# First expert's weights used whole in float32, and squares and casts issued a step or two later, in an attention, expert and gated-network kernel

## The chip, the cores and the metric

The kernel runs on one NeuronCore of a Trainium2 chip. The metric is the device time of one execution in microseconds (us). The engines are TensorE (PE; its weight loads are the row PEld), VectorE (DVE), ScalarE (ACT), GpSimd (POOL) and SyncE (SP, which here issues most of the DMAs).

## The reference: what is computed

Three stages in a row, float32 in and out.

```python
# 1. attention, B=2, H=8, S=576, D=64, causal, with a decay bias from s
scores = q @ k.T / sqrt(D) + min(-(cum[i] - cum[j]), 0)     # cum = cumsum(max(s, 0))
x = softmax(scores) @ v                                      # then 1152 tokens of 512
# 2. eight experts, top 1, capacity 288
expert = argmax(x @ w_gate); gate = softmax(x @ w_gate)[expert]
y = gate * (relu(x @ w1[expert]) @ w2[expert])               # w1 512x1024, w2 1024x512
# 3. gated network
h = y @ w_in                                                 # 512x2048
out = (h * sigmoid(h)) @ w_out                               # 2048x512
```

## The kernel before, in words

**Precision.** PE multiplies float16 here, and accuracy is kept by splitting: each float32 matrix is scaled by a power of two and split into a float16 part (hi, a cast) and the float16 rest (lo, one DVE instruction that scales and subtracts). A product is three float16 products: hi x hi, hi x lo, lo x hi. The scale comes from the sum of squares: ScalarE squares the matrix with a row sum (`w_norm`, line 132, and `w_norm2`, line 139), PE sums over partitions with a matrix of ones (`ones_sum`, L144), DVE reduces and makes the scale from the exponent bits (L146, L100 to L102).

**Attention and routing.** 56 items (a block of queries, a head, one or both batches) pass through a pipeline of steps: scores on PE in float32 (L346, L354), row minimum on DVE (L369), exponent on ScalarE (L387), split (L406 to L411), a transposing DMA (L419), the product with v (L438 to L454). Nine tiles of 128 tokens are then split (`r_split`), transposed on PE (`r_tr`, L530, copied by ScalarE at L531), multiplied with the gate weights (`r_logits`, L539 to L541), reduced to a one-hot of the best expert (`r_top`, L547 to L550), ranked (`r_pos`, L574; `r_rank`) and scattered by an indirect DMA into a table in DRAM that has a region for every expert (`r_scat`, L639). `tail` lists by hand what each engine does in the last part, tiles 6 to 8, in the order in which it is queued. Expert 0's window (its first W = 192 tokens, transposed) is not read back after the last scatter: it is read before, and the tokens of the last three tiles are added by one-hot matmuls (`win_start`, `win_mm`, `win_oh`, `win_add`, L628) and copied to `xw0` (L634, L636). `tail` also splits the first weight (`w_split0`, four parts, L202 on ScalarE and L203 on DVE) and the second (`w_split`, L165, L169, L171), and `warm` gives PE work without a result.

**Experts.** Sixteen weights are used in the order w1 of 0, w1 of 1, w2 of 0, w1 of 2, w2 of 1, ... (`WSEQ`), each 2 MB; a weight's place in it is j. Unit u is PE's work with weight u: four steps q = 0 to 3. In a w1 unit every step makes two blocks of 128 rows of the hidden layer (24 matmuls of 192 columns, `mm_h`, L749); in a w2 unit steps 0 and 2 make two blocks of the output each (48 matmuls, `mm_y`, L779). Results leave PSUM a step later: `post_h` (relu on ScalarE L755, lo part on DVE L756) and `post_y` (DVE scales by the gates into `ys`, L788, and ScalarE squares that with a sum, L791). `flush` issues them. Beside these steps unit u prepares weight j = u + 2 and n = u + 3, and loads weight u + 4:

```python
if q == 0: w_scale(j); flush(); hi(j) on ACT, DVE, POOL    # L185, L187
if q == 1: flush(); w_norm2(n, first half);  w_lo(j, first half)
if q == 2: flush(); w_norm2(n, second half); w_lo(j, second half)   # L139, L192
```

`hi(j)` is half on ScalarE (L185), a quarter on DVE and a quarter on POOL (L187). `unit0` is written out by itself and squares, casts and splits weight 2 (expert 0's w2). Staging buffers hold three weights (`wst` two, `wst2` one, by j mod 3), and the split ones three (`wsp` one, `wsp2` two). All engines' orders are by hand here (`manual_schedule`), and each engine works its queue in order.

**Gates.** Outputs are scaled by the gate of every token slot. `slots0` (DVE, L677 to L682) makes table rows from the totals, nine indirect DMAs on POOL gather the slots' data (`slots_g`, L685), `slots1` (DVE, at the start of unit 2, L692 to L700) makes the gates, SP writes them to DRAM (`gl`, L701) and reads them back to all partitions (`load_gates`, L890). From unit 3, step 2, on `post_y` is issued.

**Second network.** Its weights come as float64 words, which DVE converts in integer arithmetic (`c_conv`, L841 to L843); ScalarE squares them (`c_sq`, L849), `c_scale` makes the scale, POOL and DVE split (`c_split`, L872, L873). `c_tasks` makes a list of these; from unit 6 on two entries a unit are issued (`task`, in steps 0 and 3), the others between the matmuls of the second network (L1111, L1130), whose order a planner sets from modelled times.

Of the kernel before, what the change touches and what calls it, by code (L numbers as in the profile page):

```python
# [23 lines left out]
P = 128  # L24
# [3 lines left out]
W = 192  # L28
# [8 lines left out]
def moe_kernel(tc, qL, qtL, kL, vL, sL, wgL, w1L, w2L, capL, winL, woutL, out):  # L37
# [73 lines left out]
    NW = len(WSEQ)  # L111
    wd = [dict() for _ in range(NW)]
    pools = {}

    def w_load(j, part=None, q=SP):
# [3 lines left out]
        if part in (None, 0):  # L119
            pool = pools["wst2"] if j % 3 == 2 else wst_p  # L120
            wd[j]["st"] = pool.tile([P, 4096], F32, tag="wst", name="wst")
# [72 lines left out]

    def w_split0(f):

        d = wd[0]
        if f == 0:
            d["sp"] = wsp_p.tile([P, 2, 4096], F16, tag="wsp", name="wsp")
        v = d["st"].rearrange("p (k f) -> p k f", k=4)[:, :, f * 256:(f + 1) * 256]  # L200
        o = d["sp"].rearrange("p c (k f) -> p c k f", k=4)[:, :, :, f * 256:(f + 1) * 256]
        A.activation(out=o[:, 0], in_=v, func=AF.Copy, scale=d["s"])  # L202
        V.scalar_tensor_tensor(out=o[:, 1], in0=v, scalar=d["s"], in1=o[:, 0], op0=ALU.mult, op1=ALU.subtract)  # L203
# [401 lines left out]
    xw0 = cst.tile([P, 8, W], F16, name="xw0")  # L605
# [9 lines left out]
    def win_mm():  # L615
        a = win["a"]
        for k in range(4):
            pw.append(psS.tile([P, 512], F32, tag="s", name="pw"))
            PE.matmul(out=pw[k][:, 0:2 * W].rearrange("p (a w) -> p a w", w=W), lhsT=ident16,
                      rhs=a[:, 2 * k:2 * k + 2, :], start=True, stop=False)  # L620
# [4 lines left out]
    def win_add(t):  # L625
        o = oh0[:, t - T0, :]
        for k in range(8):
            PE.matmul(out=pw[k // 2][:, k % 2 * W:(k % 2 + 1) * W], lhsT=rt[t]["xh"][:, k * P:(k + 1) * P], rhs=o,  # L628
                      start=False, stop=(t == NT - 1 and k % 2 == 1))
            if t == NT - 1 and k % 2:  # L630
                j = k // 2
                src, dst = pw[j][:, 0:2 * W], xw0[:, k - 1:k + 1, :].rearrange("p a w -> p (a w)")
                if j % 2:
                    A.copy(dst, src)  # L634
                else:
                    V.tensor_copy(dst, src)  # L636
# [84 lines left out]
    def moe_phases():  # L721
# [15 lines left out]
        hh, posts, yposts = {}, [], []  # L737

        def mm_h(e, fp):
            if fp == 0:  # L740
                hh[e] = hp.tile([P, 2, 8, W], F16, tag="h", name="h")
            sp = wd[wi(("w1", e))]["sp"].rearrange("p c (k f) -> p c k f", k=4)
# [295 lines left out]
        for u in range(1, 4):  # L1038
            unit(u)
            if u == 1:  # L1040
                w_load(5)
# [391 lines left out]
```

## Time and profile before

| | us |
|---|---|
| median of 3 runs | 551.32 (548.91 to 554.57) |
| the profiled execution | 548.38 |
| its span, first to last instruction | 546.7 |
| mean granted clock of PE over the span | 0.93 |

The span is what all times of the trace are counted in; 1.7 us of the profiled execution lie around it. In the trace expert 0's first matmul starts at 156.9 us, unit 1 at 166.25, unit 2 at 179.9, the gates arrive at 204.6, the last expert matmul ends at 332.4, and the second network takes the rest. The rows further down give start and length in us; a wait is told with what released it.

### The profile page before, as it was taken

How to read it: one execution, taken by the hardware profiler on the slowest of the kernel's cores; microseconds unless marked ns; L12 is line 12 of the kernel's file. 1: busy time of each engine (PE TensorE's matmuls, PEld its weight loads, DVE VectorE, ACT ScalarE, POOL GpSimd, SP SyncE). 2: the span in 40 equal slices, each digit the busy share in tenths (PEclk: the TensorE clock that was granted, in tenths of full speed). 3: DMA queues.
4: the chain of work that ended last, by engine and by line, in shares of the span. 5: the costliest groups of instructions: out<-in, count | busy, mean ns of one | idle time of the engine just before them, and what ended most of it. 6: DMA issues, size and time to landing. Idle time of an engine off the chain costs nothing.

```text
span 546.7 us, 10734 instructions
## 1 busy us (share of the span) xinstructions
PE 450.2 (82%) x4094; PEld 364.7 (67%) x4095; DVE 391.6 (72%) x920; ACT 279.0 (51%) x500; POOL 223.2 (41%) x251
## 2 busy tenths in 40 slices
PE   0948678997686967986769897598999989999995
PEld 0735435675586966976669795264588866668885
DVE  8889579985778757879887889998567874452111
ACT  1665466974387557856845723555533245551000
POOL 9787485655127311100121105564542224562121
PEclk9979789998798997989697898899999999999999
DMA  9899999999359639896549601304032430000101
GB/s 160 225 178 215 219 215 249 244 235 232 114 195 340 239 91 313 255 381 190 186 155 233 259 1 42 114 2 155 0 118 66 161 122 1 0 1 20 59 40 58
DMA packets 97126, 83.10 MB, mean 152 GB/s; under 512 B 70112, under 2 KB 74400, under 8 KB 96816
## 3 DMA queue, kind: packets, MB, share of 16 engines
q1 hardware_dynamic: 93840, 75.50, 53.2%
q0 software_dynamic: 1728, 4.76, 2.4%
q10 hardware_dynamic: 1504, 2.13, 1.4%
q8 instruction: 33, 0.54, 0.4%
q14 instruction: 21, 0.17, 0.1%
HBM read 58.07 MB, written 7.91 MB: 121 GB/s over the span
## 4 chain that ended last, share of the span: by engine, by line
PE 38%; DVE 26%; DMA 15%; ACT 7%; issue 7%; POOL 4%; DVEq 0%; POOLq 0%; SPq 0%; ACTq 0%
PE psh L1111 13%; PE psy L1130 9%; DMA eT<-hl 7%; PE psh L749 4%; PE psy L779 4%; DVE wsp L192 4%; DMA gl<-gk 2%; ACT junk L139 2%; DVE cx L842 2%; DVE wsp L309 2%; PE pss L346 2%; DVE stg L843 2%; DVE et L369 2%; DMA stg<-in_moe_w_out_dram 2%; DVE hl L411 2%
## 5 line engine op out<-in xcount | busy, mean ns | idle before, releaser
L1111 PE MATMUL psh<-yh,win 128*128 128x384 f16 x576 | 98.3, 332 | 10.1 <-DVE r L1118 8.5
L1130 PE MATMUL psy<-wout,g 128*128 128x256 f16 x864 | 95.4, 273 | 3.7 <-ACT ot L1138 2.5
L1130 PEld LDWEIGHTS <-g 128*128 128x128 f16 x864 | 84.5, 98 | 14.0 <-issue 4.1
L1111 PEld LDWEIGHTS <-win 128*128 128x128 f16 x576 | 57.3, 100 | 49.9 <-issue 8.4
L749 PE MATMUL psh<-xw,wsp 128*128 128x192 f16 x768 | 75.5, 265 | 1.1 <-DVE h L756 1.1
L749 PEld LDWEIGHTS <-wsp 128*128 128x128 f16 x768 | 72.4, 108 | 2.4 <-DMA xw<-table 1.3
L192 DVE SCALAR_TENSOR_TENSOR wsp<-wst,sci,wsp 128x2048 f16<-128x2048 f32 x28 | 65.5, 2344 | 4.5 <-POOL wsp L187 2.8
L779 PE MATMUL psy<-h,wsp 128*128 128x192 f16 x768 | 68.3, 251 | 0.4 <-DVE wsp L192 0.4
L779 PEld LDWEIGHTS <-wsp 128*128 128x128 f16 x768 | 66.0, 101 | 0.9 <-DVE wsp L192 0.7
L346 PE MATMUL pss<-kt,qa 65*128 65x128 f32 (+3 forms) x128 | 51.2, 549 | 18.5 <-DMA kt<-wsp 12.4
L1120 POOL TENSOR_TENSOR g<-r,g 128x384 f16<-128x384 f32 x48 | 46.8, 978 | 43.7 <-ACT g L1119 42.2
L187 POOL TENSOR_SCALAR wsp<-wst,sci 128x1024 f16<-128x1024 f32 x13 | 15.5, 1196 | 109.7 <-DVE sci L102 60.5
L1118 DVE SCALAR_TENSOR_TENSOR r<-psh,sg 128x384 f32<-128x384 f32 x48 | 26.4, 553 | 32.4 <-ACT sg L1116 31.1
L139 ACT ACTIVATE junk<-wst 128x2048 f16<-128x2048 f32 x26 | 49.4, 1898 | 0.1
L411 POOL TENSOR_TENSOR hl<-et,hl 128x512 f16<-128x512 f32 (+3 forms) x34 | 37.7, 1116 | 18.0 <-ACT hl L406 15.3
L346 PEld LDWEIGHTS pss<-kt,qa 128*128 128x128 f32 (+1 forms) x128 | 26.3, 251 | 28.0 <-POOL qa L261 12.0
L387 ACT ACTIVATE et<-et,nm 128x128 f32<-128x128 f32 (+3 forms) x64 | 32.8, 554 | 21.4 <-DVE nm L369 21.4
L1119 ACT CAST g<-r 128x384 f16<-128x384 f32 x48 | 24.4, 510 | 33.0 <-DVE r L1118 33.0
L185 ACT ACTIVATE wsp<-wst,sci 128x2048 f16<-128x2048 f32 x14 | 27.9, 1996 | 23.2 <-DVE sci L102 17.7
L1140 DVE SCALAR_TENSOR_TENSOR ot<-psy,inv,ot 128x256 f32<-128x256 f32 x18 | 8.7, 484 | 37.4 <-PE psy L1130 37.4
L872 POOL TENSOR_SCALAR win<-stg,sci 128x512 f16<-128x512 f32 x16 | 15.7, 998 | 48.1 <-DVE sci L102 48.1
L369 DVE CUSTOM_DVE_ANT_0 et<-pss,mk 128x128 f32<-128x128 f32 (+3 forms) x64 | 28.9, 480 | 3.7 <-POOL hl L411 3.2
(247 smaller groups left out, 839.2 us busy)
## 6 DMA issues: line engine op xcount, KB each, us to landing
wst<-in_moe_w_dram SPq DMA_DIRECT2D x61, 512.0 KB, 5.9
stg<-in_moe_w_in_dram SPq DMA_DIRECT2D x16, 512.0 KB, 5.8
stg<-in_moe_w_out_dram SPq DMA_DIRECT2D x16, 512.0 KB, 4.9
table<-xh SPq DMA_DIRECT2D x4, 774.0 KB, 6.1
wst<-in_v_dram SPq DMA_DIRECT2D x2, 1024.0 KB
kt<-in_k_dram SPq DMA_DIRECT2D x3, 512.0 KB, 8.4
qa<-in_q_dram SPq DMA_DIRECT2D x3, 512.0 KB, 7.2
wst<-in_moe_w_dram ACTq DMA_DIRECT2D x3, 512.0 KB, 3.2
```

The lines of the kernel that those rows point to most:

```text
L139: A.activation(out=pools["junk2"], in_=d["st"][:, h * 2048:(h + 1) * 2048], func=AF.Square, accum_out=d["ss"][:, h:h + 1])
L185: A.activation(out=o, in_=src, func=AF.Copy, scale=d["s"])
L192: V.scalar_tensor_tensor(out=d["sp"][:, 1, lo:hi], in0=d["st"][:, lo:hi], scalar=d["s"], in1=d["sp"][:, 0, lo:hi], op0=ALU.mult, op1=ALU.s ...
L346: PE.matmul(out=pv[:, j, :], lhsT=qa[c % 2][r, h, b, :], rhs=kt[r, h, b, 0:n], start=True, stop=True)
L369: maxi[i] = V.tensor_tensor_reduce(out=ev[:, j, :], in0=st[i]["s"][:, j, :], in1=mk[:, 512 - n:512], scale=-0.125, scalar=3.0e38, op0=ALU. ...
L387: A.activation(out=e[:, j, :], in_=e[:, j, :], func=AF.Exp, scale=-1.0, bias=st[i]["m"][j])
L411: spl[i] = (V if LO[i] == "V" else G).tensor_tensor(out=hl[:, w:w + n], in0=e, in1=hl[:, 0:n], op=ALU.subtract)
L749: PE.matmul(out=pv[:, j, :], lhsT=sp[:, cw, k, a], rhs=xw[e][:, 4 * cx + k, :], start=(n == 0 and k == 0), stop=(n == 2 and k == 3))
L779: PE.matmul(out=pv[:, j - js[0], :], lhsT=sp[:, cw, k, a], rhs=hh[e][:, ch, k, :], start=(n == 0 and k == 0), stop=(n == 2 and k == 7))
L1111: PE.matmul(out=ps[:, 0:CH], lhsT=wv[:, cw, k, fo * P:(fo + 1) * P], rhs=yh[:, cy, k, a], start=(i == 0 and k == 0), stop=(i == 2 and k == 3))
L1120: G.tensor_tensor(out=gt[n][:, 1, f, :], in0=r, in1=gt[n][:, 0, f, :], op=ALU.subtract)
L1130: PE.matmul(out=o, lhsT=gt[n][:, cg, k, a], rhs=woutt[h][:, cw, k, d], start=(m == 0 and k == 0), stop=(m == 2 and k == 7))
```

## The change

The first expert's two weights (places 0 and 2, `WHOLE`) are no longer squared, scaled, cast and split. They are loaded into buffers of the split weights' pools and multiplied as they are, in float32: 4 matmuls for a block of the hidden layer instead of 12, and 8 for a block of the output instead of 24. `xw0` and the hidden layer of expert 0 are float32, `win_mm` and `win_add` sum hi and lo of the window into one PSUM region, and the copies out of it are two instead of four. Since weight 2 no longer takes a staging buffer, weight 3 is loaded where weight 2 was, weight 2 later, and weight 5 in unit 0 instead of after unit 1.

In all units the cast `hi(j)` is issued in step 1 instead of 0, the halves of `w_lo(j)` in steps 2 and 3 instead of 1 and 2, and the first half of `w_norm2(n)` in step 0 instead of 1. The square of an output is issued by a list of its own, `late`, at least one step after its scaling, and the square of a conversion one task later than its conversion.

```diff
+    WHOLE = (0, 2)
...
+            if j in WHOLE:
+                t = (wsp_p if j == 0 else pools["wsp2"]).tile([P, 2, 4096], F16, tag="wsp", name="wsp")
+                wd[j]["st"] = t.rearrange("p c f -> p (c f)").bitcast(F32)
...
-    def w_split0(f):
...
-    xw0 = cst.tile([P, 8, W], F16, name="xw0")
+    xw0 = cst.tile([P, 4, W], F32, name="xw0")
...
         def mm_h(e, fp):
...
+                if e == 0:
+                    for k in range(4):
+                        PE.matmul(out=pv[:, j, :], lhsT=sp[:, k, a], rhs=xw0[:, k, :], start=(k == 0), stop=(k == 3))
+                    continue
...
         def post_h(e, fp, pv):
+            if e == 0:
+                A.activation(out=whole_h()[:, 2 * fp:2 * fp + 2, :], in_=pv, func=AF.Relu)
+                return
...
         def mm_y(e, dp):
...
+                    if e == 0:
+                        for k in range(8):
+                            PE.matmul(out=pv[:, j - js[0], :], lhsT=sp[:, k, a], rhs=whole_h()[:, k, :],
+                                      start=(k == 0), stop=(k == 7))
+                        continue
...
             V.scalar_tensor_tensor(out=o, in0=pv, scalar=KY[:, e:e + 1], in1=g, op0=ALU.mult, op1=ALU.mult)
+            late.append((now[0], lambda: post_y2(e, d, n)))
+
+        def post_y2(e, d, n):
+            o = ys[:, d:d + n, ds(offv[e], W)]
...
         def c_tasks(m, j):
-            t = []
+            t = [[] for _ in range(5)]
             for q in range(4):
-                t.append([lambda q=q: c_conv(m, j, q), lambda q=q: c_sq(m, j, q)])
-            t.append([])
+                t[q].append(lambda q=q: c_conv(m, j, q))
+                t[q + 1].append(lambda q=q: c_sq(m, j, q))
...
-            for p in posts, yposts:
-                while p and (p is posts or gates) and (not keep or p[0][0] < now[0]):
+            for p in posts, yposts, late:
+                while p and (p is not yposts or gates) and (not keep or p[0][0] < now[0] - (p is late)):
...
             step(0, 0)
-            w_load(3, 1, A)
-            w_load(3, 2)
-            w_load(3, 3)
+            for q in range(1, 4):
+                w_load(2, q)
             for t in range(NT):
                 slots_g(t)
-            w_norm(2, 2)
-            w_norm(2, 3)
             w_load(4)
             step(0, 1)
             flush()
+            w_norm2(3, 0)
+            w_load(5)
             step(0, 2)
-            w_scale(2)
             flush()
-            w_hi(2, 0, 2048, A)
-            w_hi(2, 2048, 4096, V)
+            w_norm2(3, 1)
             step(0, 3)
             flush()
-            w_lo(2, 0, 2048)
-            w_norm2(3, 0)
-            w_norm2(3, 1)
-            w_lo(2, 2048, 4096)
...
                 flush()
-                if q == 0 and j < NW:
+                if q == 0 and n < NW:
+                    w_norm2(n, 0)
+                if q == 1 and j < NW:
                     w_hi(j, 0, 2048, A)
                     w_hi(j, 2048, 3072, V)
                     w_hi(j, 3072, 4096, G)
-                if q == 1:
-                    if n < NW:
-                        w_norm2(n, 0)
-                    if j < NW:
-                        w_lo(j, 0, 2048)
                 if q == 2:
                     if n < NW:
                         w_norm2(n, 1)
                     if j < NW:
-                        w_lo(j, 2048, 4096)
+                        w_lo(j, 0, 2048)
+                if q == 3 and j < NW:
+                    w_lo(j, 2048, 4096)
...
-        w_split0(0)
...
-        w_split0(1)
...
-        w_split0(2)
...
-        w_split0(3)
-        w_load(2, 2, A)
-        w_norm(2, 0)
+        w_load(3, 2, A)
```

## Rows read from the trace of the kernel before

**Rows 1.** The page, part 1: busy us (share of the span) and instructions.
```profile
PE 450.2 (82%) x4094; PEld 364.7 (67%) x4095; DVE 391.6 (72%) x920; ACT 279.0 (51%) x500; POOL 223.2 (41%) x251
```

**Rows 2.** Windows: start:end, length, busy by engine, PE clock, DMA share, GB/s.
```profile
139.50:145.20 5.70, 5.57 (x48) 4.40 (x47) 3.96 (x19) 2.52 (x4) 0.00 (x0) 0.50 0.24 91
...
217.70:318.70 101.00, 83.05 (x888) 81.04 (x889) 82.64 (x116) 63.78 (x88) 13.81 (x13) 0.88 0.71 225
318.70:332.30 13.60, 13.60 (x168) 13.60 (x166) 11.92 (x25) 5.63 (x17) 0.00 (x0) 1.00 0.01 1
...
351.00:450.00 99.00, 92.20 (x701) 68.78 (x702) 76.17 (x137) 47.34 (x108) 41.82 (x43) 0.98 0.25 86
```

**Rows 3.** Waits of the whole span: us in total, times, longest.
```profile
ACT stg L849 <- DVE stg L843: 35.4, 21, 5.9
...
PE psn L144 <- ACT junk L139: 29.2, 9, 7.2
...
ACT junk L791 <- DVE yg L788: 21.1, 14, 5.1
```

**Rows 4.** Chain that ended last, in the tail: start us, us, what.
```profile
137.37 1.28 DVE wsp L203
...
146.69 1.18 DVE wsp L203
...
150.98 1.16 ACT wsp L202
152.17 1.28 DVE wsp L203
```

**Rows 5.** Timeline of POOL, the first of nine gathers.
```profile
164.93 1.02 POOL L685 DMA_INDIRECT meta<-table,srow  x1 [4.54 <-DVE srow L682]
```

**Rows 6.** Chain that ended last, from the last gather to unit 7.
```profile
180.04 0.95 POOL meta L685
...
186.50 0.24 DVE gk L700
186.76 13.44 DMA gl<-gk
200.25 4.38 DMA yg<-gl
...
208.59 0.60 PE psn L144 x2
...
237.55 7.90 DMA wst<-in_moe_w_dram
```

**Rows 7.** Timeline of PE: start, us, operation, count [idle before].
```profile
12.74 4.26 PE L346 MATMUL pss<-kt,qa 65*128 65x128 f32 x19
...
96.33 2.82 PE L346 MATMUL pss<-kt,qa 128*128 128x512 f32 x6
...
104.17 2.26 PE L354 MATMUL pss<-kt,qa 128*128 128x288 f32 x8
...
139.63 0.17 PE L574 MATMUL psm<-oh,tri 128*128 128x8 f16 x1 [2.36 <-DVE oh L550]
...
156.91 6.10 PE L749 MATMUL psh<-xw,wsp 128*128 128x192 f16 x72
```

**Rows 8.** Groups of DVE from 217.7 to 318.7: busy us, mean ns, idle before.
```profile
L192 DVE SCALAR_TENSOR_TENSOR wsp<-wst,sci,wsp 128x2048 f16<-128x2048 f32 x18 | 42.2, 2344 | 0.4 <-ACT wsp L185 0.4
L187 DVE TENSOR_SCALAR wsp<-wst,sci 128x1024 f16<-128x1024 f32 x9 | 12.3, 1368 | 0.0
L756 DVE SCALAR_TENSOR_TENSOR h<-psh,h 128x384 f16<-128x384 f32 x19 | 10.5, 552 | 6.6 <-ACT h L755 6.6
L788 DVE SCALAR_TENSOR_TENSOR yg<-psy,KY,yg 128x384 f32 x9 | 5.6, 618 | 0.1
```

**Rows 9.** Waits from 217.7 to 318.7 us.
```profile
PE psn L144 <- ACT junk L139: 18.0, 6, 7.2
...
DVE sc L146 <- PE psn L144: 6.9, 6, 2.5
```

More of the change, by code (lines that the diff above doesn't have):

```diff
@@ L119, in w_load @@
         if part in (None, 0):
-            pool = pools["wst2"] if j % 3 == 2 else wst_p
-            wd[j]["st"] = pool.tile([P, 4096], F32, tag="wst", name="wst")
+            if j in WHOLE:
+                t = (wsp_p if j == 0 else pools["wsp2"]).tile([P, 2, 4096], F16, tag="wsp", name="wsp")
+                wd[j]["st"] = t.rearrange("p c f -> p (c f)").bitcast(F32)
+            else:
+                pool = pools["wst2"] if j % 3 == 2 else wst_p
+                wd[j]["st"] = pool.tile([P, 4096], F32, tag="wst", name="wst")
         v = wd[j]["st"].rearrange("p (a f) -> p a f", a=n)
@@ L193, in w_lo @@
                                in1=d["sp"][:, 0, lo:hi], op0=ALU.mult, op1=ALU.subtract)
-    def w_split0(f):
[L197 to L203, printed above, removed]
     actx = ExitStack()
@@ L616, in win_mm @@
         a = win["a"]
-        for k in range(4):
+        for k in range(2):
             pw.append(psS.tile([P, 512], F32, tag="s", name="pw"))
-            PE.matmul(out=pw[k][:, 0:2 * W].rearrange("p (a w) -> p a w", w=W), lhsT=ident16,
-                      rhs=a[:, 2 * k:2 * k + 2, :], start=True, stop=False)
+            for c in range(2):
+                PE.matmul(out=pw[k][:, 0:2 * W].rearrange("p (a w) -> p a w", w=W), lhsT=ident16,
+                          rhs=a[:, 4 * c + 2 * k:4 * c + 2 * k + 2, :], start=(c == 0), stop=False)
     def win_oh(t):
@@ L626, in win_add @@
         o = oh0[:, t - T0, :]
[L627 to L633, printed above, removed]
+        for i, k in enumerate((0, 1, 4, 5, 2, 3, 6, 7)):
+            c = k % 4
+            PE.matmul(out=pw[c // 2][:, c % 2 * W:(c % 2 + 1) * W], lhsT=rt[t]["xh"][:, k * P:(k + 1) * P], rhs=o,
+                      start=False, stop=(t == NT - 1 and i % 4 == 3))
+            if t == NT - 1 and i % 4 == 3:
+                j = i // 4
+                src, dst = pw[j][:, 0:2 * W], xw0[:, 2 * j:2 * j + 2, :].rearrange("p a w -> p (a w)")
+                if j:
+                    V.tensor_copy(dst, src)
+                else:
                     A.copy(dst, src)
-                else:
-                    V.tensor_copy(dst, src)
     def r_scat(t):
@@ L736, in moe_phases @@
         wint = [win_p.tile([P, 2, 2, 2048], F16, name=f"win{i}") for i in range(2)]
-        hh, posts, yposts = {}, [], []
+        hh, posts, yposts, late = {}, [], [], []
         def mm_h(e, fp):
@@ L1005, in unit @@
             e = WSEQ[u][1]
-            if u + 4 < NW:
-                w_load(u + 4) if u > 1 else None
+            if u + 4 < NW and u > 1:
+                w_load(u + 4)
             if WSEQ[u][0] == "w1" and 1 <= e < E - 1:
@@ L1046, in moe_phases @@
         extra += [[lambda: c_load("in", 0)]] + c_tasks("in", 0) + [[]]
-        extra += [[lambda: c_load("in", 1)], [lambda: c_load("out", 0)], []] + c_tasks("in", 1)[0:4]
+        extra += [[lambda: c_load("in", 1)], [lambda: c_load("out", 0)], []] + c_tasks("in", 1)[0:5]
         for u in range(4, NW):
@@ L1269, in early @@
                     w_load(j, s - WL[j])
-            if WL[j] + 5 <= s < WL[j] + 9:
+            if WL[j] + 5 <= s < WL[j] + 9 and j not in WHOLE:
                 w_norm(j, s - WL[j] - 5)
-            if s == WL[j] + 8:
+            if s == WL[j] + 8 and j not in WHOLE:
                 w_scale(j)
@@ L1296, in tail @@
         win_start()
-        w_load(2, 0)
-        w_load(2, 1)
+        w_load(3, 0)
+        w_load(3, 1)
         i_pv(49)
@@ L1346, in tail @@
         r_top(8)
-        w_load(3, 0)
+        w_load(3, 3)
         r_pos(8)
```

20 lines of the change are left out of this document (14 added, 6 removed).

## The prediction

> **What bounds the kernel now.** The page's first part comes first: PE is busy for 82% of the span, VectorE (DVE) for 72%, ScalarE (ACT) for 51% [rows 1]. No engine is full, so the loss is in waits, and the windows tell where. In the body of the expert stage (217.7 to 318.7 us, units 5 to 13) DVE works 82.6 of 101.0 us and PE 83.1, at a granted clock of 0.88; the last 13.6 us are PE alone, full and at 1.00 [rows 2]. Third, the list of waits. PE's largest is its weight-norm matmul (L144) waiting for ScalarE's squares of weights (L139): 29.2 us in 9 waits. ScalarE itself sits 21.1 us in front of the squares of outputs (L791) and 35.4 us in front of the squares of conversions (L849), each time for a DVE result issued in the same step [rows 3]. So a wait of ScalarE for DVE becomes one of PE, since the weight squares are queued behind it. Last, the chain of waits. Ahead of the experts it runs through expert 0's split (L202 on ScalarE, L203 on DVE) [rows 4]; then through nine gathers on POOL, the gate write (13.44 us) and its broadcast (4.38 us), to 204.7, when the first output can be scaled, and through L144 at 208.59 [rows 5, 6].
>
> **The tail before expert 0.** Four ScalarE casts and four DVE splits of expert 0's first weight go. Three places of them are on the path. The split at 137.37 stands in DVE's queue ahead of tile 6's routing: PE waited 2.36 us for its one-hot [rows 4, 7]. Right after that wait the granted clock is 0.50 (1.2 of 2.4 GHz) from 139.5 to 145.2, while PE is full (5.57 us) [rows 2]; without the wait I take these matmuls at 1.00, half of it: 2.7 us. The split at 146.69 costs 1.2 us ahead of tile 8's split. Cast and split from 150.98 to 153.45 stand ahead of tile 8's routing, whose logits are there some 1.5 us before the split ends. The window is copied out of PSUM in two pieces instead of four: 0.4 us. Sum 2.4 + 2.7 + 1.2 + 1.5 + 0.4 = 8.2; I take 8. If the clock falls all the same it is 5.5, and it can hardly be more than 8.5: what comes late next is the transposes of the attention weights, which nothing here touches. Expert 0 then starts at 148.9 instead of 156.9.
>
> **Float32 products.** A float32 matmul leaves two records. Start to start (a row's length less that of its last record, over the rest), records of 288 columns come every (2.26 - 0.41)/7 = 0.265 us and of 512 every (2.82 - 0.59)/5 = 0.446, so 0.81 ns a column; 192 columns make 0.265 - 96 x 0.81 ns = 0.187 us. Records of 128 columns with 65 rows come every (4.26 - 0.42)/18 = 0.213, which would make 0.265 for 192 [rows 7]. A unit of expert 0 is 32 float32 matmuls, 64 records: 12.0 us by the first, 17.0 by the second. The 96 float16 records it replaces take 96 x (6.10 - 0.25)/71 = 7.9. I take 12.0, the price of records that use all 128 rows as these do: 4.1 us more in each of two units, 9.1 as the upper end. Expert 0's units then end at 160.9 and, after unit 1, at 181; unit 3 ends at 189, the first half of unit 4 at 193.
>
> The Trainium skill speaks against this edit: "TensorE: Matmul & The Clock Gate", section "Weight-path perf modes", says that float32 weights get no fast load, and its section on what overlaps says that a load runs beside a matmul only when the row groups differ. By its section "LDWEIGHTS", 128 columns / 1.2, a load is 107 ns (an estimate by that page); with 192 x 0.81 = 156 ns of streaming a record would take 263 ns and a unit 17 us. The 288-column records disagree: of their 265 ns, 233 are streaming at that price, so only 32 are left for a load. The 65-row records agree (213 ns, 104 of them streaming). It is the third rival below.
>
> **The gates.** The nine gathers start once DVE has made the rows from the totals, right behind the tail, and hold POOL from 164.93 to 181.0 [rows 5, 6]; all move with the tail, by 8 us (5.5 to 8.5, as it does). POOL's cast of weight 3 stays behind them, and with it DVE's second half of that split, but this now ends at 176.6 (174.2 when the cast is done, plus 2.34 [rows 8]), ahead of the gathers' landing near 178. So the gates leave at 178.8, not 186.76, and with the same 13.44 + 4.38 us arrive at 196.7. That expert 0's second weight is neither squared, cast nor split is worth nothing by itself: units 1 and 2 gain, but PE waits at 193 for the gates in any case. This wait of some 4 us also swallows most of the float32 price.
>
> **Units 3 to 5.** Output squares a step or two later let the weight squares go ahead of them, so PE does not wait at L144 (208.59 now): its second half of unit 4 starts at 197.4, when the first output is scaled. DVE, which sat idle behind that scaling, has then to do: two scalings (1.1), four half splits (9.2), two output splits (1.0), scale and cast (1.5), offset and scaling (0.9): 13.8 us, so it stands at 210.5 where it stood at 217.7: 7 us ahead.
>
> **Units 5 to 13.** DVE's own work is unchanged: 82.6 us, over half of it the 18 half splits of 2344 ns [rows 2, 8]. Its idle time there is 18.4 us: 6.9 for the norm matmul on PE, which waited 18.0 for ScalarE [rows 9], 6.6 for relus [rows 8], the rest small. With squares later and the first weight square a step earlier PE's wait mostly goes; DVE's cast of the next weight is a step later too and finds its scale ready. What comes next is DVE itself; a full DVE holds ScalarE at the cast (its scale comes from DVE), and the second weight square is behind it. I leave 10 us idle (5 at best, 18.4 if the coupling stays): 210.5 + 82.6 + 10 = 303, against 318.7. PE's 9 units of 8 us fit in that.
>
> **The end.** After the last split PE now has 13.6 us left, as it is itself late by half a unit [rows 2]; it needs one unit, 8 us. I take 4 of the 5.5. **Second network:** there the squares of conversions a step later free ScalarE, but PE is already busy 92.2 of 99.0 us from 351 to 450 [rows 2]: 1.5 us, bounds 4 gained and 2 lost, since this part's order is laid by a planner. **Attention:** four weight squares fewer on ScalarE, hidden by DVE and transposes: nothing.
>
> Sum: 7 (lead at unit 5) + 8.4 (DVE's idle) + 4 (end) + 1.5 = 20.9. The profiled execution took 548.38 us (span 546.7): 527.5. The median of the runs shown is 551.32, 2.9 above it, so I forecast 530 for a median.
>
> **Rivals.**
> First, the coupling stays: ScalarE's cast now waits in the second step for DVE's scale, and the weight square behind it holds PE as before. The same DVE-ScalarE waits under another line speak for it; against it that the first square is already done by then. Only the 7 us and perhaps 1 elsewhere come: 543.
> Second, slower: the weight stream. The second half split moves to the fourth step, and only it frees the buffer into which the weight three places on is loaded; the first square of that weight is wanted a step sooner. Both together take two steps, 4 to 8 us, from a load whose last part already shows as 7.90 us on the chain at 237.55 [rows 6]. It decides once a load lands behind the square's new place: ScalarE, then PE, stand there in each of nine units. At 3 us a unit that is 27 against 20.9 gained: 557. Against it: a load has a whole unit, 8 us or more, between release and use.
> Third, float32 loads are not hidden: 17 us a unit puts the first half of unit 4 at 203 instead of 193, past the gates; 6 us late there, of which the full DVE further on hides some: 535.
>
> **How the numbers follow.** Forecast 0.62, first rival 0.18, third 0.10, second 0.06, and 0.04 for a planner's order in attention or the second network that takes 5 us or more. Best bounds (5 us more from DVE, 1.5 from the end, 2.5 from the second network) give 521; the upper end is the first rival's 543. About 1% (5.5 us) is what a measurement of this kernel can tell from no change. Only the second rival, and the bad ends together (tail 2.5, idle 8.4, end 4, second network 3.5), come near 551: faster 0.92, same 0.04, slower 0.04.
>
> **What would show it.** Right: expert 0's first matmul near 149; its float32 records 0.19 us apart; gates written near 179 and landed near 197; next to no wait of PE for L139; DVE over 85% busy from unit 5 to the last split; second network as long as now. Wrong: PE still waiting at L144, now for a cast (first rival); a square or cast released by a weight load (second); records 0.27 apart (third); or the gathers not moving with the tail, since then the lead of 7 us is gone and with it a third of the sum.

## The result, and the profile after

The changed kernel takes 534.02 us (median of 4 runs, 531.75 to 537.09) against 550.21 for the kernel before: ratio 0.970, 95% interval 0.962 to 0.978, 16.2 us less. Forecast were 530, inside 521 to 543. The execution that was profiled was the longest of the four (537.09 us, span 535.4), and that of before one of the shortest (548.38), so the two traces differ by 11.3 us only.

The page, part 1, answers to [rows 1]:

```profile
PE 448.2 (84%) x4026; PEld 363.7 (68%) x4027; DVE 377.9 (71%) x900; ACT 264.4 (49%) x478; POOL 217.1 (41%) x251
```

Windows, for [rows 2]: weights 7 to 15 being split (units 5 to 13), PE's rest after the last split, and the seam with the second network.

```profile
215.80:304.70 88.90, 81.43 (x945) 80.21 (x943) 81.73 (x118) 62.95 (x89) 14.24 (x13) 0.96 0.81 256
304.70:315.10 10.40, 10.40 (x127) 10.25 (x125) 10.01 (x21) 2.46 (x7) 0.00 (x0) 1.00 0.01 2
315.10:334.00 18.90, 9.83 (x47) 5.56 (x47) 18.90 (x41) 7.60 (x22) 12.43 (x12) 0.73 0.35 112
```

The first stretch took 101.0 us; DVE's work in it is nearly the same (82.6 before, 81.7 now), its idle time fell from 18.4 to 7.2, and the granted clock rose from 0.88 to 0.96. The gain is here. In the third DVE is busy without a pause: it now sets the end.

Waits of the whole span, for [rows 3]:

```profile
ACT stg L876 <- DVE stg L870: 33.3, 19, 5.6
...
ACT junk L145 <- DMA wst<-in_moe_w_dram: 14.5, 4, 8.8
...
PE psn L150 <- ACT junk L145: 11.0, 5, 3.8
...
PE psy L802 <- PEq L936: 7.1, 1, 7.1
...
ACT junk L818 <- DVE yg L811: 6.0, 2, 3.4
```

PE's wait for weight squares fell from 29.2 to 11.0, ScalarE's for outputs from 21.1 to 6.0. Two lines are new: ScalarE waits for weight loads (in L145), and PE stops once for 7.1 us at the branch (L936, the `If` of `rest`, L909 before).

Timeline of PE, for [rows 7]: start, length, operation, count [idle before].

```profile
151.89 10.64 PE L751 MATMUL psh<-xw,wsp 128*128 128x192 f32 x64
...
196.26 4.12 PE L802 MATMUL psy<-h,wsp 128*128 128x192 f16 x48
...
202.39 0.92 PE L802 MATMUL psy<-h,wsp 128*128 128x192 f16 x9 [1.86 <-DVE yg L811]
210.37 4.89 PE L802 MATMUL psy<-h,wsp 128*128 128x192 f16 x39 [7.07 <-PEq L936]
215.10 2.14 PE L755 MATMUL psh<-xw,wsp 128*128 128x192 f16 x24
```

Expert 0 starts 5.0 us earlier, its 64 float32 records take 10.64 us, and unit 5 starts at 215.10 instead of 215.48: the lead of 7 us that was forecast is missing in this trace. Timelines of ScalarE, POOL and DVE between the two, for [rows 5, 6]:

```profile
171.84 1.91 ACT L145 ACTIVATE junk<-wst 128x2048 f16<-128x2048 f32 x1 [8.78 <-DMA wst<-in_moe_w_dram]
...
173.75 0.47 ACT L767 ACTIVATE h<-psh 128x384 f16<-128x384 f32 x1
```
```profile
161.30 1.02 POOL L684 DMA_INDIRECT meta<-table,srow  x1 [2.57 <-DVE srow L681]
...
171.45 0.95 POOL L684 DMA_INDIRECT meta<-table,srow  x1 [0.30 <-issue]
```
```profile
174.25 0.56 DVE L768 SCALAR_TENSOR_TENSOR h<-psh,h 128x384 f16<-128x384 f32 x1 [7.88 <-ACT h L767]
...
179.72 2.34 DVE L198 SCALAR_TENSOR_TENSOR wsp<-wst,sci,wsp 128x2048 f16<-128x2048 f32 x1
...
183.55 0.24 DVE L699 SCALAR_TENSOR_TENSOR gk<-fin,capf,meta 128x9 f32<-128x9 f32 x1
...
201.72 1.14 DVE L811 SCALAR_TENSOR_TENSOR yg<-psy,KY,yg 128x384 f32 x2 [6.88 <-DMA yg<-gl]
```

In unit 1 ScalarE stands 8.78 us before the square of weight 4, whose load is under way; relu, DVE's lo part, the split of weight 3 and the gates are queued behind. DVE makes the gates (L699) 3.0 us earlier than before, and the first scaling is 3.0 earlier too.

### The profile page after: what moved, and what is told of

Read it like the earlier page. It is cut to its first block, busy times and chain, and to the rows that moved or that the text cites. A ratio compares the mean times of both kernels' runs of the same rounds, so it can differ in the third digit from the quotient of the medians.

```text
span 535.4 us, 10546 instructions
## 1 busy us (share of the span) xinstructions
PE 448.2 (84%) x4026; PEld 363.7 (68%) x4027; DVE 377.9 (71%) x900; ACT 264.4 (49%) x478; POOL 217.1 (41%) x251
## 4 chain that ended last, share of the span: by engine, by line
DVE 22%; PE 22%; DMA 8%; issue 5%; ACT 1%; SPq 1%; POOL 0%; POOLq 0%; DVEq 0%; ACTq 0%
PE psh L1127 11%; PE psy L1146 9%; DVE wsp L198 5%; DMA stg<-in_moe_w_out_dram 4%; DVE cx L869 4%; DVE stg L870 3%; DMA stg<-in_moe_w_in_dram 3%; DVE cx L868 2%; DVE win L900 2%; DVE yh L1091 1%; DVE r L1134 1%; DVE h L768 1%; DMA wst<-in_moe_w_dram 1%; PE psy L802 1%; DVE wout L900 1%
## 5 line engine op out<-in xcount | busy, mean ns | idle before, releaser
L1146 PE MATMUL psy<-wout,g 128*128 128x256 f16 x864 | 97.2, 275 | 4.5 <-ACT ot L1154 3.1
L802 PE MATMUL psy<-h,wsp 128*128 128x192 f16 x672 | 58.9, 249 | 8.9 <-PEq L936 7.1
L802 PEld LDWEIGHTS <-wsp 128*128 128x128 f16 x672 | 56.9, 100 | 9.5 <-issue 7.3
L755 PE MATMUL psh<-xw,wsp 128*128 128x192 f16 x672 | 61.5, 255 | 1.1 <-DMA xw<-table 0.9
L198 DVE SCALAR_TENSOR_TENSOR wsp<-wst,sci,wsp 128x2048 f16<-128x2048 f32 x26 | 60.4, 2344 | 0.6 <-ACT wsp L191 0.6
L755 PEld LDWEIGHTS <-wsp 128*128 128x128 f16 x672 | 59.2, 103 | 2.1 <-DMA xw<-table 1.2
L145 ACT ACTIVATE junk<-wst 128x2048 f16<-128x2048 f32 x26 | 49.5, 1904 | 14.6 <-DMA wst<-in_moe_w_dram 14.5
L342 PEld LDWEIGHTS pss<-kt,qa 128*128 128x128 f32 (+1 forms) x128 | 27.4, 259 | 28.4 <-POOL qa L257 12.2
L383 ACT ACTIVATE et<-et,nm 128x128 f32<-128x128 f32 (+3 forms) x64 | 32.8, 554 | 27.6 <-DVE nm L365 27.5
L407 POOL TENSOR_TENSOR hl<-et,hl 128x512 f16<-128x512 f32 (+3 forms) x34 | 36.0, 1067 | 15.2 <-ACT hl L402 9.9
L191 ACT ACTIVATE wsp<-wst,sci 128x2048 f16<-128x2048 f32 x13 | 26.0, 1999 | 19.8 <-DVE sci L102 11.1
L365 DVE CUSTOM_DVE_ANT_0 et<-pss,mk 128x128 f32<-128x128 f32 (+3 forms) x64 | 28.9, 480 | 8.3 <-POOL hl L407 8.0
```

Of the source, the lines that this page charges most:

```text
L145: A.activation(out=pools["junk2"], in_=d["st"][:, h * 2048:(h + 1) * 2048], func=AF.Square, accum_out=d["ss"][:, h:h + 1])
L198: V.scalar_tensor_tensor(out=d["sp"][:, 1, lo:hi], in0=d["st"][:, lo:hi], scalar=d["s"], in1=d["sp"][:, 0, lo:hi], op0=ALU.mult, op1=ALU.s ...
L342: PE.matmul(out=pv[:, j, :], lhsT=qa[c % 2][r, h, b, :], rhs=kt[r, h, b, 0:n], start=True, stop=True)
L365: maxi[i] = V.tensor_tensor_reduce(out=ev[:, j, :], in0=st[i]["s"][:, j, :], in1=mk[:, 512 - n:512], scale=-0.125, scalar=3.0e38, op0=ALU. ...
L383: A.activation(out=e[:, j, :], in_=e[:, j, :], func=AF.Exp, scale=-1.0, bias=st[i]["m"][j])
L407: spl[i] = (V if LO[i] == "V" else G).tensor_tensor(out=hl[:, w:w + n], in0=e, in1=hl[:, 0:n], op=ALU.subtract)
```

## The experiments

Four marks are read from the timelines of PE and DVE in every profile: the first matmul of expert 0 (E); the start of DVE's last step for the gates, right ahead of their write, from E on (G); the 18 half splits of weights 7 to 15 (units 5 to 13), from the end of weight 6's split (U); and from the last of these to the end of the span (R). us; the ratios are to the kernel before, run in the same series.

| kernel | E | G | U | R | median | ratio (95%) |
|---|---|---|---|---|---|---|
| before | 156.9 | 29.6 | 101.1 | 227.9 | 550.2 | |
| changed | 151.9 | 31.7 | 88.9 | 230.7 | 534.0 | 0.970 (0.962 to 0.978) |
| e1_order | 159.8 | 29.8 | 86.9 | 230.2 | 538.6 | 0.976 (0.970 to 0.982) |
| e2_f32 | 146.7 | 28.8 | 101.4 | 233.5 | 547.6 | 0.991 (0.987 to 0.996) |
| e7_sqnow | 147.3 | 30.9 | 99.4 | 230.4 | 543.6 | 0.986 (0.977 to 0.994) |
| e10_csq | 154.0 | 30.3 | 93.9 | 231.3 | 544.1 | 0.986 (0.982 to 0.991) |
| e8_unitold | 153.7 | 27.5 | 92.7 | 231.9 | 538.7 | 0.978 (0.972 to 0.984) |
| e3_norm1 | 150.7 | 28.7 | 87.8 | 229.9 | 531.4 | 0.961 (0.954 to 0.968) |
| e12_norm1 | 151.8 | 30.6 | 90.0 | 231.4 | 534.3 | 0.970 (0.964 to 0.976) |
| e4_rest5 | 151.1 | 31.3 | 90.6 | 229.3 | 537.6 | 0.975 (0.967 to 0.983) |
| e5_nobranch | 146.7 | 31.2 | 85.3 | 227.6 | 528.6 | 0.960 (0.951 to 0.970) |
| e9_both | 151.5 | 30.6 | 86.6 | 231.4 | 535.7 | 0.972 (0.967 to 0.976) |
| e6_end | 150.7 | 31.7 | 89.3 | 229.1 | 533.3 | 0.966 (0.958 to 0.973) |
| e11_same | 147.3 | 30.4 | 89.0 | 231.6 | 533.1 | 0.966 (0.961 to 0.971) |

Two kernels stand here twice: the changed one (and e11_same) has U at 88.9 and 89.0, e3_norm1 and e12_norm1 have 87.8 and 90.0. A difference of 2 us in U tells nothing.

**The change in two halves.** e1_order is the kernel before with the order edits alone:

```diff
+            late.append((now[0], lambda: post_y2(e, d, n)))
...
-                t.append([lambda q=q: c_conv(m, j, q), lambda q=q: c_sq(m, j, q)])
...
+                t[q].append(lambda q=q: c_conv(m, j, q))
+                t[q + 1].append(lambda q=q: c_sq(m, j, q))
...
-            for p in posts, yposts:
...
+            for p in posts, yposts, late:
...
-                if q == 0 and j < NW:
+                if q == 0 and n < NW:
+                    w_norm2(n, 0)
+                if q == 1 and j < NW:
                     w_hi(j, 0, 2048, A)
...
```

> The kernel before with the order edits alone: cast a step later, both half splits a step later, first weight square a step earlier, output squares by the late list, conversion squares a task later; expert 0 is still split into float16. Theory A (the gain of units 5 to 13 is the order's): that stretch is 88 to 91 us instead of 101.0, the wait of PE for the weight squares under 12 us in all, and the time 540 to 544 if the second network is again some 6 us longer, 535 to 538 if it is not. Theory B (the gain comes from the work that expert 0 no longer makes, and its lead runs through): that stretch stays near 101 and the time within 3 us of before.

e2_f32 is the changed kernel with these hunks taken back; `WHOLE`, the tail and the loads stay.

> The change without its order edits: expert 0 whole in float32 with its tail and its loads, but cast, splits, weight squares, output squares and conversion squares issued as before. Theory A: expert 0 starts near 152, the gates are written near 180 (the first square of weight 4 stands behind step 1's relu here, so its wait for the load does not hold that relu), units 5 to 13 stay near 100, and the time is 3 to 7 us under before. Theory B: most of the 16 us of the change come here, time 534 to 538.

Theory A holds in both, with misses: U of e1_order is under the 88 to 91 expected, and e2_f32 starts expert 0 at 146.7, not 152. The order edits alone bring 2.4% (U 86.9; its interval, 1.8 to 3.0%, does not settle whether that is over 2%); the float32 expert alone brings 0.9% and leaves U at 101.4. The two add up to 3.3%, and the change has 3.0. Windows of e1_order, then of e2_f32:

```profile
221.70:308.60 86.90, 78.72 (x899) 76.94 (x897) 81.52 (x117) 61.67 (x87) 14.22 (x13) 0.96 0.85 261
```
```profile
206.70:308.10 101.40, 84.44 (x889) 81.92 (x889) 82.70 (x117) 63.82 (x88) 13.76 (x13) 0.88 0.72 224
```

In e2_f32 the split of weight 6 ended at 206.7, 11 us earlier than before, and none of it shortened U: a lead is carried through that stretch, not multiplied.

**Which order edit.** Three kernels, each the changed one with one edit undone. e7_sqnow squares an output at once:

```diff
-            late.append((now[0], lambda: post_y2(e, d, n)))
+            post_y2(e, d, n)
```

> The changed kernel, but every output square is issued right behind its scaling again, as before. Theory A as predicted (the late squares let the weight squares go first): units 5 to 13 rise from 88 by 3 to 7 us, and ScalarE waits some 10 to 20 us for scalings again. Rival (with the cast a step later and the first square earlier, the place of the output squares no longer matters): that stretch stays within 1 us of 88, and the time falls by up to 2 us, since the sum of squares at the end is made earlier.

e10_csq squares a conversion in its own task:

```diff
-            t = [[] for _ in range(5)]
+            t = []
...
-                t[q].append(lambda q=q: c_conv(m, j, q))
-                t[q + 1].append(lambda q=q: c_sq(m, j, q))
+                t.append([lambda q=q: c_conv(m, j, q), lambda q=q: c_sq(m, j, q)])
...
```

> The changed kernel, but the square of a conversion is issued in the same task as the conversion again. Theory A (in the second network this edit is worth nothing, since DVE sets the pace there): from the last half split to the end 228 to 232 us as with it; units 5 to 13 within 1.5 us of 88.8, or longer by 1 to 4 us if ScalarE's weight squares wait behind the conversions' squares in units 6 to 13; the time 0 to 4 us over the change. Rival (the late conversion squares are what lengthened the second network): last half split to the end 225 to 228, time 2 to 4 us under.

e8_unitold puts cast, half splits and the first weight square into their old steps:

```diff
-                if q == 0 and n < NW:
-                    w_norm2(n, 0)
-                if q == 1 and j < NW:
+                if q == 0 and j < NW:
                     w_hi(j, 0, 2048, A)
...
+                if q == 1:
+                    if n < NW:
+                        w_norm2(n, 0)
+                    if j < NW:
+                        w_lo(j, 0, 2048)
...
```

> The changed kernel, but in the units cast, half splits and first weight square stand in their old steps; output and conversion squares stay late. Theory A (both halves of the reordering are needed, the larger part being that of cast, splits and squares): units 5 to 13 take 94 to 99 us, time 6 to 10 us over the change. Rival (the late output squares alone do it): 87 to 90 us, time within 2 us of the change.

Undone one at a time, the three cost U 10.5, 5.0 and 3.8 us, together more than the 12.2 that all are worth. So the output squares are the largest part: e7_sqnow lost more than its theory A expected (3 to 7), and e8_unitold less (92.7, not 94 to 99), where the larger part had been put down to cast, splits and first weight square. That the sum is more than the whole fits one chain, ScalarE's queue, in which an early instruction that waits for DVE holds the weight squares behind it. That chain is argued from the waits. Waits of e7_sqnow from 211.2 to 310.6, then of e10_csq from 217.3 to 311.3; in the changed kernel from 215.8 to 304.7 the two last lines of each pair are 7.5 (L876) and 7.2 us (L150):

```profile
ACT junk L818 <- DVE yg L811: 23.3, 8, 7.3
...
PE psn L150 <- ACT junk L145: 15.0, 6, 3.8
```
```profile
ACT stg L876 <- DVE stg L870: 12.8, 4, 6.6
...
PE psn L150 <- ACT junk L145: 9.2, 2, 5.1
```

In e8_unitold it is the cast (L191) that waits for DVE's scale: 26.7 us from 214.6 to 307.25, 13.6 in the changed kernel, with 10.9 us of PE at L150.

For e10_csq both theories fell short. The late conversion squares are worth about 2% (0.986 against 0.966 of e11_same in the same series), and the place is units 6 to 13, where four conversions stand among the weights' work. In the second network (R 231.3, 231.6 in e11_same) they are worth nothing. U shows 5 of the 11 us between the medians; where the other 6 lie is not shown. (The two profiles differ by 6.7 in E, which no edit touches.)

**The gates.** e3_norm1 moves one square, in unit 1:

```diff
-                if q == 0 and n < NW:
+                if q == (2 if u == 1 else 0) and n < NW:
                     w_norm2(n, 0)
```

> The changed kernel, but in unit 1 alone the first half square of weight 4 is issued in step 2 instead of step 0. Theory A (that square, waiting 8.8 us for its load, holds the relus, weight 3's split and so the gates): no relu waits behind it, the gates are written at 177.5 to 180 instead of 183.8, the first scaling starts 4 to 6 us earlier than 201.7, and the time falls by 2 to 5 us. Rival: the gathers and the cast on POOL behind them (end 173.6) hold the gates anyway: written after 182, time within 1 us of the change.

> The changed kernel with the first half square of weight 4 in unit 1's step 2, run again with more rounds. If what its first run showed holds (gates some 2 us earlier after expert 0's first matmul, everything behind them with them): ratio to before 0.958 to 0.965, median 528 to 532. If that run was only a short one among executions that differ by some 5 us: ratio 0.966 to 0.972, as the changed kernel.

No square stands ahead of the first two relus any more, and in the first run G is 28.7 instead of 31.7. In the second it is 30.6 and the ratio that of the changed kernel, so the time cannot be told from the change's. The traces tell two kinds of executions apart. In unit 1 of all eight profiles from e5 to e12 PE has four to eight gaps, 3.7 to 5.3 us in all, in which it waits for nothing that the profile shows; in the first profile of the changed kernel, in before and in e1 to e4 there are none. Without the gaps the early square goes with a G of 31.3 and 31.7, its move with 28.7: about 3 us. With them it is 30.3 to 31.7 against 30.6 (e9_both, e12_norm1), and no gain can be told. The early square is not all: G is lowest with all the old steps (27.5 in e8_unitold, 28.8 in e2_f32). There weight 3's cast and split, which stand ahead of the gates on DVE, are issued a step earlier; these alone were not tried.

**The branch.** e4_rest5 issues it behind unit 5:

```diff
-        for u in range(1, 4):
+        for u in range(1, 6):
             unit(u)
         man.close()
...
-        for u in range(4, NW):
+        for u in range(6, NW):
             unit(u)
```

> The changed kernel, but the branch for experts of more than 192 tokens stands after unit 5 instead of after unit 3. Theory A (the branch is a meeting point where PE waits until the vector engine has worked off its queue): the second half of unit 4 runs through without the 7.1 us stop, and unit 5 starts on PE near 207 to 209 instead of 215; since the vector engine sets the pace from there, the time falls by 0 to 3 us. Rival (PE waits there for a buffer or a result of unit 4, not for the branch): the stop stays at the same matmul, unit 5 starts at 214 to 216.

The stop goes with the branch. PE, then DVE of e4_rest5:

```profile
217.36 0.58 PE L802 MATMUL psy<-h,wsp 128*128 128x192 f16 x5
225.34 4.57 PE L802 MATMUL psy<-h,wsp 128*128 128x192 f16 x35 [7.40 <-PEq L936]
```
```profile
220.24 0.56 DVE L768 SCALAR_TENSOR_TENSOR h<-psh,h 128x384 f16<-128x384 f32 x1 [0.26 <-DVEq L936]
```

Unit 4 runs through, unit 5 starts at 206.96, and the stop is now in unit 6, as long as ever, though DVE passed the branch 5 us before PE went on. So PE does not wait for DVE's backlog there, as theory A had it; my theory was wrong in its mechanism. Nothing is won (U 90.6), since behind the stop DVE waits 6.56 us for PE's norm matmul. e5_nobranch leaves out `rest()`, the code for experts of more than 192 tokens, which these inputs do not enter:

```diff
         flush(0)
-        rest()
```

> The changed kernel without the branch behind unit 3, that is, without the code for experts of more than 192 tokens, which these inputs do not enter. Theory A (at the branch PE's sequencer stands still for 5 to 7 us, wherever the branch is and whatever the other engines do, as in the run with the branch after unit 5): PE goes through the second half of unit 4 without a stop and is 7 us ahead at unit 5 (near 208); DVE's time from there hardly changes, so the total falls by 0 to 3 us. Rival (the stop was a wait for DVE's backlog): a stop of 4 us or more stays near the same matmuls.

The stop is gone. Timeline of PE of e5_nobranch:

```profile
192.24 4.12 PE L802 MATMUL psy<-h,wsp 128*128 128x192 f16 x48
196.20 0.31 PE L150 MATMUL psn<-sc,ones 128*128 128x2 f32 x2
196.57 4.13 PE L802 MATMUL psy<-h,wsp 128*128 128x192 f16 x48
203.83 3.73 PE L755 MATMUL psh<-xw,wsp 128*128 128x192 f16 x24 [3.12 <-DMA xw<-table]
```

U falls to 85.3, with 81.5 of DVE's work in it: about half of the idle time that the change left there goes with the branch, in this one profile. The time is some 5 us lower, with intervals that overlap. The branch does not always make a stop, though: in e1_order and e7_sqnow, which have it, PE goes over it in 0.30 us and runs on, and in e3_norm1 and e12_norm1 the stop (5.61 and 6.14 us) comes one matmul behind it. e9_both tries for that with the branch kept:

```diff
             for q in range(4):
+                if (u, q) == (3, 2):
+                    man.close()
+                    rest()
+                    man2.enter_context(tc.manual_schedule(engines=ME))
                 step(u, q)
...
-        man.close()
         flush(0)
-        rest()
-        man2.enter_context(tc.manual_schedule(engines=ME))
```

and with the edit of e3_norm1.

> The changed kernel with the first half square of weight 4 in unit 1's step 2 and the branch issued between steps 1 and 2 of unit 3, where PE's stop for it falls before its wait for the gates. Theory A (the two losses are separate and add): PE stops 5 to 7 us in the middle of unit 3 near 186, the gates are written 27.5 to 29 us after expert 0's first matmul, the second half of unit 4 follows the first scaling without a second stop, units 5 to 13 take 85 to 88 us as without the branch, and the time is 5 to 9 us under the changed kernel of the same series. Rival (only the lead of PE comes, and DVE's pace hides it): units 5 to 13 stay at 88 to 89 and the time falls by 2 to 4 us, as with the square alone.

Part of it came: U is 86.6 and there is no second stop. But the time is 535.7, not below the 533.1 of e11_same. Timeline of PE of e9_both:

```profile
168.43 0.33 PE L755 MATMUL psh<-xw,wsp 128*128 128x192 f16 x2 [0.99 <-issue]
169.90 0.24 PE L755 MATMUL psh<-xw,wsp 128*128 128x192 f16 x1 [1.15 <-issue]
170.61 0.24 PE L755 MATMUL psh<-xw,wsp 128*128 128x192 f16 x1 [0.47 <-issue]
172.02 5.85 PE L755 MATMUL psh<-xw,wsp 128*128 128x192 f16 x34 [1.16 <-issue]
...
197.91 6.02 PE L755 MATMUL psh<-xw,wsp 128*128 128x192 f16 x48 [5.15 <-PEq L936]
```

In this execution unit 1 lost 4 us in five of the gaps told of above (one lies ahead of these rows), and G is 30.6, not the 27.5 to 29 expected. Their cause was not found. No version here beats the changed kernel for certain.

**The seam with the second network.** In the changed kernel the first matmul of the second network follows the last expert matmul by 9.8 us, where it was 3.3 before. DVE, changed kernel: the sum of output squares, and the scale made from it in three small steps, spread by conversions and splits that the planner put between them.

```profile
318.57 0.16 DVE L1079 TENSOR_REDUCE yt<-ysq 128x1 f32<-128x18 f32 x1
...
321.67 0.14 DVE L100 TENSOR_SCALAR sci<-psn 128x1 int32<-128x1 int32 x1
321.74 1.13 DVE L900 SCALAR_TENSOR_TENSOR win<-stg,sci,win 128x512 f16<-128x512 f32 x1
...
324.12 0.14 DVE L101 TENSOR_SCALAR sci<-sci 128x1 int32<-128x1 int32 x1
```

e6_end closes it up:

```diff
-            late.append((now[0], lambda: post_y2(e, d, n)))
+            if e == E - 1:
+                post_y2(e, d, n)
+            else:
+                late.append((now[0], lambda: post_y2(e, d, n)))
...
                     for f in extra.pop(0):
-                        f()
+                        if left[0] > 0:
+                            left[0] -= 1
+                            with tc.issue_after(got.ins):
+                                f()
+                        else:
+                            f()
```

(`got` is the last instruction of that scale; the first ten of `extra` are held.)

> The changed kernel with two edits at the seam between experts and second network: the last expert's output squares are issued at once, and the first ten conversions, squares, scales and splits behind it wait until the scale of the expert outputs is made. Theory A (late squares and the planner's order each delay the first matmul of the second network): the sum of squares is reduced 1.4 us after the last expert matmul instead of 3.4, the first matmul of the second network stands 3 to 5 us behind it instead of 9.8, and the time falls by 3 to 6 us. Rival (the second network is bound by its conversions and splits on DVE, so that an early start is lost in a later wait): the first matmul is as early, but the stretch to the end stays within 1.5 us of 220 and the time within 1.5 us.

The rival holds. Timeline of PE of e6_end:

```profile
319.31 9.90 PE L1139 MATMUL psh<-yh,win 128*128 128x384 f16 x48 [1.13 <-ACT yh L1095]
335.41 16.23 PE L1139 MATMUL psh<-yh,win 128*128 128x384 f16 x84 [6.20 <-DVE r L1146]
```

The first matmul is 4.8 us closer, and the wait comes back as 6.20 us one group later. R is 229.1 and the time as without the edit. The sum of squares came hardly earlier (3.1 us behind the last matmul): on ScalarE five output squares, the last of them a late one of the expert before, and a conversion square still stood in one row from 313.95 to 317.3.

**The same kernel again.**

> The changed kernel itself once more, to be compared with its variants on the same chip. If executions of the same instructions differ by some 5 us ahead of expert 0, as the profiles so far let it appear, its first matmul of expert 0 lies anywhere from 146 to 153 us in this profile; the stretch of units 5 to 13 is 88 to 90 us, and the median 531 to 537.

All three held: E 147.3, U 89.0, median 533.07 (ratio 0.966). Windows of 100 to 146 us, in attention and tail, of the first profile of the changed kernel, then of this one:

```profile
100.00:146.00 46.00, 40.15 (x471) 32.15 (x469) 35.64 (x133) 24.95 (x45) 22.00 (x33) 0.89 1.03 229
```
```profile
100.00:146.00 46.00, 40.99 (x524) 32.88 (x523) 36.28 (x153) 27.87 (x50) 22.85 (x32) 1.00 1.05 250
```

The same instructions ran at a granted clock of 0.89 in one and 1.00 in the other, and expert 0 started 4.6 us apart. The three kernels at 1.00 (e2_f32, e5_nobranch, e11_same) have E at 146.7 to 147.3; the eight at 0.89 to 0.93 have 150.7 to 154.0. (e7_sqnow, at 0.96, has 147.3.)

## Why the prediction was right, and by which of its steps

The measured time lies in the range, though not every sign came: the gates were written at 184.2 and first used at 201.7 us (179 and 197 forecast), and PE still waits 11.0 us for the weight squares (next to none forecast). The first rival's wait is there, the cast for DVE's scale, 13.6 us in units 5 to 13, but DVE's idle time fell by 11.2 us all the same.

**The tail: 8 forecast, 8.1 on average, 6.4 at a like clock.** With the float32 expert E is 150.3 in the mean of twelve profiles; without it, in the two there are, 156.9 and 159.8: 8.1 less. PE's two long waits for one-hots (2.36 and 1.78 us, in both of these) are gone in all twelve, and its idle time from 120 us to expert 0 is 10.3 us before and 3.1 after. The term that did not come as put is the clock's (2.7): nine of the twelve still have a stretch at 0.50 (1.2 GHz) between 128 and 143 us. The bound of 5.5, "if the clock falls all the same", is the better one there: the eight profiles at 0.89 to 0.93 from 100 to 146 us have 151.9 in the mean, 6.4 less than the two without, which are at 0.89 and 0.91. The profiled one is among the eight, hence 5.0 in the trace.

**Float32 records: 0.187 us forecast, 0.164 measured start to start (10.64 us a unit, not 12.0).** The mis-sized term is 1.4 us a unit, on the good side. The 288-column row that it was taken from has eight records; the longest row of the kernel before has 24:

```profile
114.77 6.07 PE L354 MATMUL pss<-kt,qa 128*128 128x288 f32 x24
```

Its records come every (6.07 - 0.41)/23 = 0.246 us, not 0.265, and less 96 x 0.81 ns that makes 0.168. The third rival (0.265) is false: the rule of the Trainium skill it rested on ("TensorE: Matmul & The Clock Gate", section "Weight-path perf modes") does not cost time here. The 65-row records that were read as bearing it out ([rows 7], 0.213) ran at the lower clock level: that trace has no granted clock ahead of 23.1 us, where it shows a rise to 1.00 with PE full, and the 256-column records around that moment come every 0.427 us up to it and every 0.216 behind it. So these ran at 1.2 GHz, and nothing tells that a load cost them time. At 2.4 GHz 128 columns would take about 0.107 (an estimate, half of 0.213).

**The gates: forecast 29.9 us from expert 0 to the write, measured 30.9 to 32.3 where the early square stands.** (G, which ends ahead of the write, is 0.6 less.) The step that failed is the one that let only the gathers hold them. The last gather ended at 172.4, 8.6 us earlier than before, but weight 3's split, forecast to end at 176.6, ended at 182.1. The square of weight 4, moved a step ahead, met its load still on the way and held ScalarE for 8.78 us, and with it relu and split. That is the second rival's mechanism, in one unit; in units 5 to 13 ScalarE waited for weight loads only 1.7 us, so that rival did not decide.

**Units 3 to 5.** "So PE does not wait at L144" came true, "its second half of unit 4 starts at 197.4" did not: it began at 202.39, after the first scaling, and stood from 203.31 to 210.37 at the branch. PE goes over the branch in unit 4 in the kernel before too. The two steps of its sequencer (PEldq) there, before and then after (length in ns, then first and last start in us):

```profile
L909 PEldq EVENT_SEMAPHORE  x2: 51/51/51, 202.7 to 202.8; - x2
```
```profile
L936 PEldq EVENT_SEMAPHORE  x2: 51/51/51, 203.5 to 210.3; - x2
```

Before, PE was over the branch by 202.9 and then stood at L144 until the square's end at 208.55 (start 208.59). So that wait was the square's, as [rows 6] has it; the stop at the branch is another one, which the kernel before does not show. It is not what cost the lead: DVE sets the pace here, and the 13.8 us that it was to work behind the first scaling were 14.1. DVE stood at 215.9 instead of 210.5, since that scaling came at 201.7 instead of 196.7: 3.0 us for expert 0's start, the rest for the gates. So only 1.8 us of the lead of 7 show in the profiled pair. Over all profiles the end of weight 6's split is 6.6 us earlier with the float32 expert (213.04, mean of twelve) than without (219.68, of two); that is a mean over kernels with other edits, and the changed kernel's own two profiles have 215.9 and 209.3.

**Units 5 to 13: 8.4 forecast, 12.2 measured.** The mechanism was right; the term of "10 us idle" was too large: it is 7.2, and 5.4 in e1_order (the other 0.9 us is DVE's work, 82.6 before and 81.7 after). The price of the three edits was laid out wrongly, though. The waits in front of conversion squares (L849) were put down to the second network alone; four of them stood in units 6 to 13, and moving these is worth 5.0 of U. What the higher granted clock (0.96, not 0.88) gave back in that was not tried by itself.

**The end and the second network: 5.5 forecast, 2.8 lost.** From the last split to the end it is 227.9 before and 227.6 to 233.5 in the other thirteen profiles. PE's rest did shrink, from 13.6 to 10.4 us, but DVE was the limit: after the last split it works 30.8 of 32.5 us before and 28.9 of 29.3 after. Windows, before and then after:

```profile
318.70:351.20 32.50, 24.08 (x219) 19.34 (x217) 30.79 (x65) 12.75 (x32) 11.99 (x12) 0.94 0.20 65
```
```profile
304.70:334.00 29.30, 20.23 (x173) 15.80 (x172) 28.91 (x61) 10.06 (x28) 12.43 (x12) 0.83 0.23 73
```

A shorter rest of PE only bared DVE's conversions. The 2.8 themselves are within what this stretch varies by: e2_f32, without the order edits, has the longest. The step that failed read the end off PE's row in [rows 2] and not off DVE's beside it. Of the planner's rival (0.04) this is not a case: closing the seam by hand gained nothing.

By the steps, with the lead from the means: 6.6 (lead) + 12.2 (units) - 2.8 (end) = 16.0, and the medians differ by 16.2. That the two meet so closely is partly chance, as the lead is a mean over other kernels and the other two are from one pair of profiles. Forecast were 20.9; the 4.9 short are the end's 8.3 and the lead's 0.4, less the 3.8 that the units gave beyond the forecast. That two steps missed in opposite directions, and the total came near for it, is luck; that most of the gain came from DVE's idle time in units 5 to 13 is not.

## What to carry to other kernels

A square or any side sum issued right behind its producer makes its engine wait in order, and everything queued behind it waits too. Issuing such squares a step late, with the casts and splits beside them, cost no instruction and was worth 12 us here, and all of them had to move: output squares left early gave 10.5 of it back, conversion squares 5.0. An instruction issued earlier is worth something only if its input is there: the square moved ahead of its load held the gates. Before a gain at the end of a stage is counted, look which engine is full there: DVE's row, not PE's, told that the end would not move. And a wait that is taken away can bare another at the same place, as PE's stop at the branch did.

## What was not expected of the hardware

- The granted clock from 100 to 146 us was anything from 0.89 to 1.00 in the twelve float32 profiles, for the same instructions, and with it expert 0 started up to 7 us apart. Two single profiles of this kernel can't settle 5 us; a stretch that begins behind the spread, as U, can.
- Around a branch whose code is not entered PE stopped for 5.15 to 7.40 us in nine of thirteen profiles (in two of them one matmul behind it), and not in before, e1_order, e2_f32 and e7_sqnow. DVE, where the trace shows a pause for it, went over it in 0.26 to 0.30. In the nine another engine's branch instruction starts within 1 us of PE's, in the four none within 2.4; whether that is the cause was not tried.
- PE's unit 1 has gaps of 3.7 to 5.3 us in all without a wait in eight profiles and none in the other six, some of which run the same kernel. Their cause is open.
- Float32 records of 192 columns by 128 rows, each with a weight load of its own, came every 0.164 us at a granted clock of 1.00.
